# Sharing idle V columns between steps, leaving out the idle lane, and a new order of work, in a two-lane transformer kernel on TensorE

## The chip, the cores and the metric

The kernel runs on one core of one Trainium2 chip. The metric is the device time of a run in microseconds (us).

Engines in the views: PE is TensorE's matmuls, PEld its weight loads, DVE is VectorE, ACT is ScalarE, POOL is GpSimd, SP issues the transfers.

## The reference, cut to what matters

```python
def _A_ref(x, wqkv, wo):         # 32 heads of 18; token s sees s, s-2, ... s-14 (8 places)
    logits = jnp.einsum('bhsd,bhswd->bhsw', q, kg) * scale
    attn = _softmax(logits)
    o = jnp.einsum('bhsw,bhswd->bhsd', attn, vg)
    return o @ wo
def _B_ref(x, mem0, Wq, Wk, Wv, Wo, seg_len):   # 32 heads of 128, segments of 32, memory of 8
    mem = mem0
    for s in range(n_seg):                      # 64 segments, one after another
        h = concatenate([mem, x[segment s]])    # 40 tokens
        o = softmax(q k' * scale, masked) v @ Wo
        mem = o[:, :8]; outs.append(o[:, 8:])
x = A_x                                         # 2048 tokens of 576
x = x + _A_ref(_layernorm(x), A_wqkv, A_wo)
x = x + _B_ref(_layernorm(x), ...)
x = x + _A_ref(_layernorm(x), A_wqkv, A_wo)
x = x + _B_ref(_layernorm(x), ...)
```

The memory makes layer B serial: a segment needs the memory tokens that the segment before it has made.

## The kernel before

The two B layers run side by side as two "lanes", lane 1 six segments behind lane 0. One step `t` treats one segment of each lane: 80 columns in `hT`, in the order x of lane 0 (32), memory of lane 0 and of lane 1 (16), x of lane 1 (32). There are 70 steps; the first six have lane 0 alone, the last six lane 1 alone. The 64 tiles of layer A (64 tokens each) fill the gaps. A planner in the program simulates the engines with given durations and fixes the order of every engine's instructions from the priorities given with each operation.

Layer A has no matmul for its local attention: GpSimd multiplies q with eight shifted k into a large tile `big`, TensorE sums over channels, and after the softmax the weights are spread over the channels again ("spread"), evicted into `big`, multiplied by v on VectorE and added up, mostly on GpSimd.

```python
# tile of layer A: the product on GpSimd
def prod(e, c0=c0, nb=nb):
    self.tt(e, big.t[:, c0:c0 + nb], qT.t[...].to_broadcast([P, nb, AW, T]), win(kT.t, c0, nb), ALU.mult)
o = pl.op("POOL", 1.0 * nb + 0.05, prod, pr(0.34 + 0.02 * n), ...)
# [cut: logits, softmax] the spread, and its evictions by ScalarE or VectorE (AD_)
ps = pl.buf("o4")
b = pl.op("PE", 0.35, lambda e, ps=ps: spread(ps, 0, 4), pr(0.55), [o], acq=[ps], ...)
for g in range(NQ):
    evs.append(pl.op(AD_, _evac(512), lambda e, g=g, ps=ps: self.copy(e, big.t[:, 0:4, :, g * 16:(g + 1) * 16],
                                                                      ps.t[:, g, :]...), pr(0.56), [b], ...))
# [cut] the first add of the products with v
o = pl.op(("POOL", "DVE"), (2.6, 0.85), lambda e: self.tt(e, big.t[:, :, 0:4], big.t[:, :, 0:4], big.t[:, :, 4:8], ALU.add), ...)
# [cut] the normalised tokens xnb; the upper half of one block is a copy of the lower
o = pl.op("DVE", 0.18, lambda e: nc.vector.tensor_copy(out=xnb.t[64:128, :, 5, :], in_=xnb.t[0:64, :, 4, :]), ...)
# a step's tokens into hT
self.x_in[t][l] = pl.op(("POOL", "DVE"), (0.45, 0.2),
    lambda e, l=l, s=s, xnb=xnb: self.copy(e, hT.t[:, :, XC[l]:XC[l] + SEG], xnb.t[:, s % NS]), ...)
# V of block b (32 of the 96 columns of hT), two halves of 20 matmuls
for r in range(2):
    ps = pl.buf("r")
    def mm(e, r=r, ps=ps):
        for kc in range(5):
            for c in range(4):
                ...  l = hT.t[:, kc, b * 32:b * 32 + 32]
                nc.tensor.matmul(ps.t[c * 32:(c + 1) * 32, :], lhsT=l, rhs=w, start=(kc == 0), stop=(kc == 4))
# softmax of a step: sums, 1/sum, product (for the memory's queries "em" on VectorE)
nc.vector.tensor_reduce(out=s, in_=v, axis=AX.X, op=ALU.add)
nc.vector.reciprocal(out=s, in_=s)
if mul == "DVE":
    nc.vector.tensor_tensor(out=v, in0=v, in1=s...to_broadcast(shp), op=ALU.mult)
```

Of the kernel before, what the change touches and what calls it, by code (L numbers as in the profile page):

```python
# [16 lines left out]
P = 128  # L17
SEG = 32
NM = 8
W80 = 80  # L20
# [10 lines left out]
AW = 8  # L31
# [163 lines left out]
class _K:  # L195
# [37 lines left out]
    def setup(self):  # L233
# [110 lines left out]
        tiles("em", 2, [P, 4, 96], zero=True)  # L344
        tiles("ex", 2, [P, 2, 4, 64], zero=True)
# [3 lines left out]
        nc.gpsimd.memset(self.OT[:], 0.0)  # L349
        self.pl.pool("OTm", [None])  # L350
        self.pl.pool("OTx", [None])
        tiles("qk", 7, [P, 3, 2, W80])
# [32 lines left out]
    def layernorm(self, xT, dep, prio, writer, wus, wacq=(), wuses=()):  # L385
# [3 lines left out]
        a = pl.op(AD_, (0.46, 0.49), lambda e: self.copy(e, xs.t[:, :, 0, :], xT.t[:]), prio, [dep], acq=[xs], uses=[xT])  # L389
# [6 lines left out]
        b = pl.op(AD_, (0.46, 0.49), square, prio, [a], uses=[xs, xT])  # L396
# [6 lines left out]
        c = pl.op("PE", 0.28, mm, prio, [b], acq=[ps], uses=[xs])  # L403
# [16 lines left out]
    def wblock(self, i, prio, dep):  # L420
        w = self.pl.buf("ring")
        o = self.pl.op("SP", 0.5, lambda e: self.nc.sync.dma_start(out=w.t[:], in_=self.wA[i]), prio, [dep], acq=[w], lat=3.2)
        return w, o

    def a_tile(self, layer, j, dep, due, span):
# [4 lines left out]
        def pr(f):  # L430
            return due - span * (1.0 - f)
        if layer == 1:
# [21 lines left out]
        gate = pl.op("NONE", 0.0, None, pr(0.1), [o_x], acq=[xn])  # L454
        o_n = self.layernorm(xT, gate, pr(0.1), wr, 1.67, wuses=[xn])
# [5 lines left out]
        for part in (0, 1, 2):  # L461
            ps = pl.buf("r")
            o = o_n
            for c in range(5):
                w, ow = self.wblock(part * 5 + c, pr(0.2) - 0.1, gate)
# [5 lines left out]
                o = pl.op("PE", 0.15, mm, pr(0.22 + 0.03 * part), [o, ow], acq=[ps, dst[part]] if c == 0 else (),  # L471
                          uses=[xn, w] if c == 0 else [xn, w, ps], lat=0.0 if c < 4 else None)
                if c == 0 and part > 0:
                    def hcopy(e, part=part):
                        h = dst[part].t[:, :, 0:HALO]
                        if first:
                            nc.gpsimd.memset(h, 0.0)
                        else:
                            nc.gpsimd.tensor_copy(out=h, in_=hin[0].t[:, part - 1])
                    got[part, "h"] = pl.op("POOL", 0.25, hcopy, pr(0.22), [o] if first else [o, hin[1]],  # L480
                                           uses=[dst[part]] if first else [dst[part], hin[0]])
# [7 lines left out]
            got[part] = pl.op(AD_, _evac(320), ev, pr(0.24 + 0.03 * part), [o], uses=[ps, dst[part]])  # L489
        if j + 1 < self.NT:  # L490
# [5 lines left out]
            oh = pl.op("POOL", 0.5, hsave, pr(0.33), [got[1], got[2]], acq=[hk], uses=[kT, vT])  # L496
# [8 lines left out]
        for n, (c0, nb) in enumerate(((0, 2), (2, 2), (4, 1))):  # L505
# [3 lines left out]
            o = pl.op("POOL", 1.0 * nb + 0.05, prod, pr(0.34 + 0.02 * n), [o] if o else [got[0], got[1], got[1, "h"]],  # L509
# [10 lines left out]
        o = o_l = pl.op("PE", 0.4, logits, pr(0.5), [o], acq=[psL, e_], uses=[big], mode="C")  # L520

        def amax(e):
            v = psL.t[:, 0:P].rearrange("p (w t) -> p w t", w=AW)
            if first:
# [3 lines left out]
        o = pl.op("DVE", 0.6, amax, pr(0.5), [o], acq=[nmx], uses=[psL])  # L528
        o = pl.op("ACT", 0.28, lambda e: nc.scalar.activation(out=e_.t[:], in_=psL.t[:, 0:P].rearrange("p (w t) -> p w t", w=AW),
                                                              func=ACT.Exp), pr(0.5), [o], uses=[psL, e_])  # L530
# [5 lines left out]
        o = pl.op("DVE", 0.9, norm, pr(0.52), [o], acq=[ssum], uses=[e_])  # L536
# [8 lines left out]
        b = pl.op("PE", 0.35, lambda e, ps=ps: spread(ps, 0, 4), pr(0.55), [o], acq=[ps], uses=[e_], mode="R")  # L545
        evs = []
        for g in range(NQ):
            evs.append(pl.op(AD_, _evac(512),
                             lambda e, g=g, ps=ps: self.copy(e, big.t[:, 0:4, :, g * 16:(g + 1) * 16],
                                                             ps.t[:, g, :].rearrange("p (c w t) -> p c w t", c=4, w=AW)),  # L550
                             pr(0.56), [b], uses=[ps, big]))
        ps = pl.buf("o4")
        b = pl.op("PE", 0.1, lambda e, ps=ps: spread(ps, 4, 1), pr(0.58), [b], acq=[ps], uses=[e_], mode="R")
        e4 = pl.op(AD_, _evac(512),
                   lambda e, ps=ps: self.copy(e, big.t[:, 4].rearrange("p w (g t) -> p g w t", g=NQ),
                                              ps.t[:, :, 0:P].rearrange("p g (w t) -> p g w t", w=AW)),
                   pr(0.6), [b], uses=[ps, big])
        mus = []
        for c0, nb in ((0, 2), (2, 2), (4, 1)):
            mus.append(pl.op("DVE", 0.15 + 0.3 * nb,  # L560
                             lambda e, c0=c0, nb=nb: self.tt(e, big.t[:, c0:c0 + nb], big.t[:, c0:c0 + nb], win(vT.t, c0, nb), ALU.mult),
                             pr(0.62), evs + [got[2], got[2, "h"]] if nb == 2 else [e4, got[2], got[2, "h"]], uses=[big, vT]))
# [3 lines left out]
                  pr(0.64), mus, uses=[big])  # L566
        o = pl.op(PD, (1.44, 0.5), lambda e: self.tt(e, big.t[:, :, 0:2], big.t[:, :, 0:2], big.t[:, :, 2:4], ALU.add),
                  pr(0.66), [o], uses=[big])
        o = o_o = pl.op(PD, (0.78, 0.33), lambda e: self.tt(e, oT.t[:], big.t[:, :, 0], big.t[:, :, 1], ALU.add),
                        pr(0.68), [o], acq=[oT], uses=[big])  # L570
        ps = pl.buf("r")
        for mb in range(5):
            w, ow = self.wblock(WOB + mb, pr(0.68) - 0.1, o_l)

            def mm(e, mb=mb, w=w, ps=ps):
                for c in range(5):
                    nc.tensor.matmul(ps.t[:, mb * T:(mb + 1) * T], lhsT=w.t[:, c, :], rhs=oT.t[:, c, :], start=(c == 0), stop=(c == 4))
            o = pl.op("PE", 0.15, mm, pr(0.72), [o, ow], acq=[ps] if mb == 0 else (),
# [3 lines left out]
                  pr(0.75), [o], uses=[ps, xT])  # L582
# [5 lines left out]
        def wr2(e, m, rstd):  # L588
# [5 lines left out]
            for o, i, bc in views:  # L594
                self.tt(e, o, i, bc(m), ALU.subtract)
                self.tt(e, o, o, bc(rstd), ALU.mult)
        o = self.layernorm(xT, o, pr(0.8), wr2, 2.1, wacq=[xnb])
        o = pl.op("DVE", 0.18, lambda e: nc.vector.tensor_copy(out=xnb.t[64:128, :, 5, :], in_=xnb.t[0:64, :, 4, :]),
                  pr(0.9), [o], uses=[xnb])
# [43 lines left out]
    def softmax(self, ps, e_, n, prio, dep, mul, view, eview, last, pt, ptpool):  # L643
# [29 lines left out]
        if mul != "DVE":  # L673
# [6 lines left out]
            "p i b q -> p (i b q)" if len(pt.t.shape) == 4 else "p l i b q -> p (l i b q)"), in_=e_.t[:].rearrange(  # L680
            "p i k -> p (i k)" if len(e_.t.shape) == 3 else "p l i k -> p (l i k)")), prio, [o], acq=[pt], uses=[e_])

    def load_x(self, t):
# [7 lines left out]
        for l in range(2):  # L691
            s = self.lane_seg(t, l)
            if s is None:
                continue
            xnb, dep = self.xn_ready[l][s // NS]
            self.x_in[t][l] = pl.op(("POOL", "DVE"), (0.45, 0.2),
                                    lambda e, l=l, s=s, xnb=xnb: self.copy(e, hT.t[:, :, XC[l]:XC[l] + SEG], xnb.t[:, s % NS]),
                                    t - 0.42, [dep, gate], uses=[hT, xnb])
            if s == 0:
# [5 lines left out]
    def qk(self, t, g, prio):  # L705
# [4 lines left out]
        hT, ps, sb = self.hT[t], pl.buf("r"), pl.buf("qk")  # L710

        def mm(e):
            pv = ps.t[:, 0:480].rearrange("p (h w k) -> p h w k", h=3, w=2)
            for hh, h in enumerate(heads):
                for wi in range(2):
                    wt, wr = self.Wb[wi]
                    for kc in range(4):
                        nc.tensor.matmul(pv[:, hh, wi, :], lhsT=wt[:, kc, h * P:(h + 1) * P], rhs=hT.t[:, kc, 0:W80],  # L718
                                         start=(kc == 0), stop=False)
                    nc.tensor.matmul(pv[:, hh, wi, :], lhsT=wr[:, (h % 16) * P:(h % 16 + 1) * P],  # L720
                                     rhs=hT.t[:, 4 + h // 16, 0:W80], start=False, stop=True)
        o = pl.op("PE", 0.358 * n, mm, prio, [*self.x_in[t].values(), *self.mem_in[t]], acq=[ps, sb], uses=[hT], tmin=TW[0])
# [3 lines left out]
        def ev(e):  # L726
            pv = ps.t[:, 0:480].rearrange("p (h w k) -> p h w k", h=3, w=2)
            self.copy(e, sb.t[:, 0:n], pv[:, 0:n])
        self.qk_ev[g] = pl.op(AD_, _evac(160 * n), ev, prio, [o], uses=[ps, sb])
        self.qkt[g] = sb  # L730

    def vpass(self, t, b, prio):

        nc, pl = self.nc, self.pl
        hT, V = self.hT[t], pl.buf(f"V{b}")
        wv, wvr = self.Wb[2]
        self.V[b] = V
        xin = [self.x_in[t][0 if b == 0 else 1]]
        gate = pl.op("NONE", 0.0, None, prio, xin, acq=[V])
        for r in range(2):  # L740
            ps = pl.buf("r")

            def mm(e, r=r, ps=ps):
                for kc in range(5):
                    for c in range(4):
                        if kc < 4:
                            l, w = hT.t[:, kc, b * 32:b * 32 + 32], wv[:, kc, (16 * r + 4 * c) * P:(16 * r + 4 * c + 4) * P]
                        else:
                            l, w = hT.t[:, 4 + r, b * 32:b * 32 + 32], wvr[:, 4 * c * P:(4 * c + 4) * P]
                        nc.tensor.matmul(ps.t[c * 32:(c + 1) * 32, :], lhsT=l, rhs=w, start=(kc == 0), stop=(kc == 4))  # L750
            o = pl.op("PE", 1.08, mm, prio, [gate] + (self.mem_in[t] if b == 1 else []), acq=[ps], uses=[hT, V],
# [4 lines left out]
    def scores(self, t, r, kind, prio):  # L756
# [6 lines left out]
        e_, pt = pl.buf("e" + kind), pl.buf("pt" + kind)  # L763
        self.e_[kind] = e_
# [5 lines left out]
        def mm(e):  # L770
# [12 lines left out]
            for l in range(1 if m else 2):  # L783
                for i in range(4):
# [251 lines left out]
```

## Time and profile before

| | before |
|---|---|
| time, median of three runs | 2670.16 us (2659.29 to 2672.51) |
| TensorE busy, share of the span | 88% |
| VectorE busy | 67% |
| GpSimd busy | 34% |
| matmuls | 73360 |
| steps with both lanes (6 to 63), per pair of steps | 72.8 us |

The last row, and all times of stretches below, come from the timeline: VectorE's copy of the new memory (`hT<-psY`) closes each step, and I take the distance of such copies.

Columns after the bar: busy time in us, mean ns of one, idle time before.

```profile
L671 DVE TENSOR_TENSOR em<-em,sum 128x320 bf16<-128x320 bf16 x140 | 71.6, 511 | 4.8
L598 DVE COPY xnb<-xnb 64x64 bf16<-64x64 bf16 x64 | 16.8, 298 | 2.9 <-POOL xnb L230 1.8
```

The typical copy in the timeline lasts 0.17 us; a mean of 298 ns says that some last longer: 20 of the 64 take over 0.4 us, most of them about 0.5. The excess adds up to some 6 us (16.8 - 64 x 0.17) in the whole run.

### The profile page before, as it was taken

The page shows a single profiled execution, that of the slowest core. Times are in us where ns is not written, and L with a number is a line of the kernel's source. Part 1 is how long each engine was busy: PE and PEld are TensorE (multiplying, and loading weights), DVE is VectorE, ACT ScalarE, POOL GpSimd, SP SyncE. Part 2 cuts the span into 40 slices and gives each one's busy share as a digit, 9 for nine tenths or more (in the row PEclk, how much of TensorE's full clock was granted, in tenths as well). Part 3 has the DMA queues.
Part 4 walks back from the last instruction along what each step waited for, and adds up shares of the span by engine and source line. Part 5 has one row for each costly group of instructions (what it writes and reads, how often), then busy time and mean ns, then how long its engine had stood idle before and what let it go on. Part 6 is the DMA issues. An engine that isn't in the chain of part 4 may idle for free.

```text
span 2673.1 us, 158511 instructions
## 1 busy us (share of the span) xinstructions
PE 2348.8 (88%) x73360; PEld 1975.7 (74%) x73360; DVE 1783.3 (67%) x4094; ACT 942.6 (35%) x2048; POOL 913.2 (34%) x1250
## 2 busy tenths in 40 slices
PE   0279899989999999999999999999999999999998
PEld 0167777777787777777787787777777777777777
DVE  1256777667777667766767676767776667676665
ACT  0022333333333334333333333434343334333322
POOL 3222333333343433333333343433333333332220
PEclk9999999999999999999999999999999999999999
DMA  7721333333333333333333333333333333322210
GB/s 257 196 85 57 101 95 88 104 105 98 100 105 114 114 114 103 97 90 107 102 111 102 100 106 114 114 114 101 95 92 103 109 104 96 103 76 62 61 42 8
DMA packets 231420, 270.45 MB, mean 101 GB/s; under 512 B 42340, under 2 KB 227236, under 8 KB 229220
## 3 DMA queue, kind: packets, MB, share of 16 engines
q1 hardware_dynamic: 227508, 241.44, 31.0%
q0 software_dynamic: 3248, 18.88, 2.0%
q8 instruction: 573, 9.39, 1.5%
q14 instruction: 91, 0.75, 0.1%
HBM read 244.10 MB, written 16.12 MB: 97 GB/s over the span
## 4 chain that ended last, share of the span: by engine, by line
PE 67%; DVE 11%; ACT 7%; DMA 6%; issue 3%; SPq 3%; POOL 2%; ACTq 0%; DVEq 0%; POOLq 0%
PE r L718 21%; PE r L750 14%; PE psY L865 12%; DMA ring<-wA_blk 6%; PE r L720 5%; PE r L469 5%; DVE big L225 3%; ACT big L223 3%; PE o L841 2%; SPq L298 2%; ACT OT L223 2%; PE o L808 2%; DVE r L659 2%; DVE nmx L658 1%; PE o L542 1%
## 5 line engine op out<-in xcount | busy, mean ns | idle before, releaser
L718 PE MATMUL r<-hT,wq 128*128 128x80 bf16 x8960 | 695.2, 202 | 0.5 <-ACT em L661 0.2
L718 PE MATMUL r<-hT,wk 128*128 128x80 bf16 x8960 | 694.9, 202 | 0.0
L750 PE MATMUL r<-wv,hT 128*32 128x512 bf16 x6720 | 447.7, 384 | 56.8 <-ACT em L661 33.6
L718 PEld LDWEIGHTS <-wq 128*128 128x128 bf16 x8960 | 461.4, 100 | 36.8 <-issue 33.2
L865 PE MATMUL psY<-OT,wo 128*128 128x80 bf16 (+1 forms) x11360 | 451.7, 202 | 19.4 <-issue 8.2
L718 PEld LDWEIGHTS <-wk 128*128 128x128 bf16 x8960 | 466.2, 100 | 0.0
L720 PE MATMUL r<-hT,wk_r 128*128 128x80 bf16 x2240 | 453.2, 202 | 0.0
L720 PE MATMUL r<-hT,wq_r 128*128 128x80 bf16 x2240 | 453.1, 202 | 0.0
L865 PEld LDWEIGHTS <-wo 128*128 128x128 bf16 x11360 | 428.4, 100 | 29.1 <-issue 27.0
L225 DVE CAST qk<-r 128x480 bf16<-128x480 f32 (+1 forms) x409 | 262.6, 642 | 259.4 <-PE r L720 256.3
L230 POOL TENSOR_TENSOR ex<-ex,sum 128x384 bf16<-128x384 bf16 x140 | 115.9, 828 | 864.5 <-DVE sum L669 790.4
L750 PEld LDWEIGHTS <-hT 128*32 128x32 bf16 x8400 | 211.1, 97 | 241.7 <-issue 84.7
L230 POOL TENSOR_TENSOR big<-qT,kT 128x1024 bf16<-128x1024 bf16 (+1 forms) x192 | 326.0, 1705 | 140.2 <-ACT kT L223 48.6
L223 ACT ACTIVATE qk<-r 128x480 bf16<-128x480 f32 (+1 forms) x361 | 200.7, 557 | 182.6 <-PE r L720 181.9
L469 PE MATMUL r<-xn,ring 128*128 128x64 bf16 x4800 | 237.4, 196 | 26.0 <-DMA ring<-wA_blk 18.0
L223 ACT ACTIVATE OT<-o 128x512 bf16<-128x512 f32 (+1 forms) x335 | 163.3, 507 | 243.0 <-PE o L841 101.5
L230 POOL TENSOR_TENSOR big<-big 128x640 bf16<-128x640 bf16 (+1 forms) x62 | 93.1, 1501 | 417.5 <-DVE big L230 407.4
L469 PEld LDWEIGHTS <-ring 128*128 128x128 bf16 x4800 | 181.5, 99 | 66.9 <-issue 33.3
L720 PEld LDWEIGHTS <-wk_r 128*128 128x128 bf16 x2240 | 224.5, 100 | 0.0
L720 PEld LDWEIGHTS <-wq_r 128*128 128x128 bf16 x2240 | 224.4, 100 | 0.0
L223 ACT ACTIVATE V<-r 128x512 bf16<-128x512 f32 x250 | 149.2, 597 | 208.5 <-PE r L750 206.8
L750 PE MATMUL r<-wv_r,hT 128*32 128x512 bf16 x1680 | 169.7, 382 | 0.8 <-issue 0.8
(137 smaller groups left out, 3501.5 us busy)
## 6 DMA issues: line engine op xcount, KB each, us to landing
ring<-wA_blk SPq DMA_DIRECT2D x1280, 160.0 KB, 3.0
x1T<-x SPq DMA_DIRECT2D x32, 160.0 KB, 3.6
x<-x1T SPq DMA_DIRECT2D x32, 160.0 KB, 2.4
x3T<-x SPq DMA_DIRECT2D x32, 160.0 KB, 3.9
x<-x3T SPq DMA_DIRECT2D x32, 160.0 KB, 3.7
wo<-in_B_Wo_dram POOLq DMA_DIRECT2D x1, 4608.0 KB, 27.5
wq<-in_B_Wq_dram POOLq DMA_DIRECT2D x4, 1024.0 KB, 10.8
wk<-in_B_Wk_dram POOLq DMA_DIRECT2D x4, 1024.0 KB, 20.1
```

Of the source, the lines that this page charges most:

```text
L223: nc.scalar.activation(out=out, in_=in_, func=ACT.Copy, scale=1.0 if scale is None else scale)
L225: (nc.vector if e == "DVE" else nc.gpsimd).tensor_copy(out=out, in_=in_)
L230: (self.nc.vector if e == "DVE" else self.nc.gpsimd).tensor_tensor(out=out, in0=in0, in1=in1, op=op)
L298: nc.sync.dma_start(out=self.wA[i], in_=wn[:, :, col0:col0 + P])
L469: nc.tensor.matmul(ps.t[:, c * T:(c + 1) * T], lhsT=w.t[:, kc, :], rhs=xn.t[:, kc, :], start=(kc == 0), stop=(kc == 4))
L659: nc.vector.tensor_tensor(out=v, in0=v, in1=m.unsqueeze(len(shp) - 1).to_broadcast(shp), op=ALU.add)
L718: nc.tensor.matmul(pv[:, hh, wi, :], lhsT=wt[:, kc, h * P:(h + 1) * P], rhs=hT.t[:, kc, 0:W80], start=(kc == 0), stop=False)
L720: nc.tensor.matmul(pv[:, hh, wi, :], lhsT=wr[:, (h % 16) * P:(h % 16 + 1) * P], rhs=hT.t[:, 4 + h // 16, 0:W80], start=False, stop=True)
L750: nc.tensor.matmul(ps.t[c * 32:(c + 1) * 32, :], lhsT=l, rhs=w, start=(kc == 0), stop=(kc == 4))
L808: nc.tensor.matmul(ps.t[:, c, i * 16:(i + 1) * 16], lhsT=V[b].t[q4, r, i, :], rhs=pt.t[q4, i, b, 0:16], start=(i == 0 and b == 0), stop=(i ...
L841: nc.tensor.matmul(o, lhsT=V[b].t[q4, r, i, :], rhs=p, start=(r == 0 and i == 0 and b == 0), stop=(r == 1 and i == 3 and b == 2), skip_gro ...
L865: nc.tensor.matmul(psY.t[:, mb, c0:], lhsT=self.wo[:, w0:w0 + P], rhs=self.OT[:, h, c0:], start=(h == 0 and mb == 0), stop=(h == NH - 1 an ...
```

## The change

Three V passes of 32 columns per step carry 80 columns of tokens: 16 columns are empty. The change puts 16 tokens of lane 0's next segment there in even steps, so that the odd step needs two passes, five per pair in place of six. Steps with one lane compute only their own columns (Q, K, scores, PV, output projection). And all priorities of the planner get new values, weights of A are requested earlier, and the spread is evicted by channel block.

```diff
@@ V passes
+    def vblocks(self, t):
+        l0, l1 = self.lanes(t)
+        if t % 2 == 0:
+            return [(0, 0) if l0 else None, (1, 32), (2, 64) if l0 or l1 else None]
+        return [(2, None) if l0 else None, (1, 16), (0, 48) if l1 else None]
...
-   l, w = hT.t[:, kc, b * 32:b * 32 + 32], wv[...]
+   l, w = hT.t[:, kc, c0:c0 + 32], wv[...]
@@ tokens of the next segment
+            if l == 0 and t % 2 == 0:
+                self.x_ahead = pl.op(("POOL", "DVE"), (0.25, 0.17), lambda e, ...:
+                                     self.copy(e, hT.t[:, :, W80:HW_], xnb.t[:, s % NS + 1, :, 0:HW_ - W80]), ...)
@@ Q and K, output projection: only the columns of the lanes that are on
+        a, b = 0 if l0 else 40, W80 if l1 else 40
...
+        c0, c1 = (0 if on[0] else MC if m else XC[1]), (W80 if on[1] else XC[1])
@@ spread of A
-        for g in range(NQ):
-            evs.append(... big.t[:, 0:4, :, g * 16:(g + 1) * 16] <- ps.t[:, g, :] ...)
+        for c in range(5):
+            if c == 4:
+                ps = pl.buf("o4")
+                b = pl.op("PE", 0.1, lambda e, ps=ps: spread(ps, 4, 1), pr(Q[4] + 0.02), [b], ...)
+            evs.append(... big.t[:, c] <- ps.t[:, :, c % 4 * P:(c % 4 + 1) * P] ..., pr(Q[4] + 0.01 * c), ...)
@@ priorities (before: numbers in place)
+PR = dict(qk=0.07, qkd=0.043, v1=0.432, v0=0.542, m0=0.196, x0=0.393, m1=0.369, x1=0.577, pm0=0.625, pm1=0.332,
+          o=0.747, od=0.01, mo=0.789, xo=1.046, px=1.007, v2=0.838, a1=0.606, a1s=3.252, a2=1.206, a2s=1.532,
+          fin=4.369, res=-0.44, ring=1.183, A=(0.005, 0.238, 0.614, 0.586, 0.529, 0.726, 0.636, 0.949))
```

(Cut: score and PV index work, wider softmax tiles, the order of heads in OT, a layernorm whose square no longer waits for its copy, memsets, durations given to the planner.)

## The prediction

> **What bounds the kernel now.** I read the head of the page first, then the costliest groups, then TensorE's waits, then one pair of steps by stretch and by time.
>
> ```profile
> span 2673.1 us, 158511 instructions
> PE 2348.8 (88%) x73360; PEld 1975.7 (74%) x73360; DVE 1783.3 (67%) x4094; ACT 942.6 (35%) x2048; POOL 913.2 (34%) x1250
> ...
> PE 67%; DVE 11%; ACT 7%; DMA 6%; issue 3%; SPq 3%; POOL 2%; ACTq 0%; DVEq 0%; POOLq 0%
> PE r L718 21%; PE r L750 14%; PE psY L865 12%; DMA ring<-wA_blk 6%; PE r L720 5%; PE r L469 5%; DVE big L225 3%; ACT big L223 3%; PE o L841 2%; SPq L298 2%; ACT OT L223 2%; PE o L808 2%; DVE r L659 2%; DVE nmx L658 1%; PE o L542 1%
> ```
>
> TensorE is busy 88% of the span, 104 us of the rest being set-up before its first matmul, and two thirds of the chain that ended last is its work. The reader is to see that it is the bound nearly everywhere, so a matmul removed should be time removed. The kernel is 70 steps of the memory layer ("B"), with the tiles of the local-attention layer ("A") as filler between. Steps 0 to 5 have only lane 0, 6 to 63 both lanes, 64 to 69 only lane 1. VectorE's copy of the new memory into hT marks the ends of steps: one stands at 1282.19 us, the next but one at 1354.86. That stretch, one pair of steps, in the view by stretches (columns: stretch, length, then busy us of PE, PEld, DVE, ACT, POOL):
>
> ```profile
> 1282.19:1354.86 72.67, 67.11 (x2124) 56.70 (x2121) 51.27 (x120) 28.16 (x62) 27.27 (x36) 1.00 0.36 103
> ```
>
> So 72.7 us a pair, DVE at 51.3 of them (71%), clock at full: no second engine is near its limit. 5.6 us per pair TensorE sits idle. The view of waits, TensorE alone, between 360 and 2440 us (28.5 pairs), says for whom (total us, times, longest):
>
> ```profile
> PE o L841 <- DVE big L225: 33.1, 28, 1.4
> PE r L750 <- ACT em L661: 31.1, 55, 1.0
> PE o L542 <- DVE big L225: 21.6, 28, 0.8
> PE o L841 <- issue: 15.4, 15, 2.1
> PE r L469 <- DMA ring<-wA_blk: 12.8, 22, 2.2
> PE r L750 <- ACT V L223: 11.7, 28, 0.4
> ```
>
> The same few waits come back in every pair: 28 and 55 times are once and twice a pair.
>
> The price of one matmul is read from the timeline, as the distance from one start to the next; the durations on the page (202 ns for one of 80 columns) overlap.
>
> ```profile
> 1341.77 1.05 PE L750 MATMUL r<-wv,hT 128*32 128x512 bf16 x16
> 1342.64 0.39 PE L750 MATMUL r<-wv_r,hT 128*32 128x512 bf16 x4
> 1342.86 0.31 PE L781 MATMUL r<-mask_m,ident 128*32 128x320 bf16 x4
> ...
> 1344.38 0.41 PE L791 MATMUL r<-qk 128*32 128x48 bf16 x32
> 1344.72 0.51 PE L808 MATMUL o<-ptm,V 32*128 32x16 bf16 x48
> 1345.19 0.31 PE L469 MATMUL r<-xn,ring 128*128 128x64 bf16 x5
> ...
> 1351.35 0.31 PE L469 MATMUL r<-xn,ring 128*128 128x64 bf16 x5
> 1351.50 0.88 PE L865 MATMUL psY<-OT,wo 128*128 128x80 bf16 x20
> ...
> 1352.51 2.31 PE L865 MATMUL psY<-OT,wo 128*128 128x80 bf16 x60
> 1354.65 0.86 PE L469 MATMUL r<-xn,ring 128*128 128x64 bf16 x15
> 1355.45 0.93 PE L841 MATMUL o<-ptx,V 32*128 32x32 bf16 x96
> 1356.31 0.47 PE L469 MATMUL r<-xn,ring 128*128 128x64 bf16 x10
> ```
>
> Half a V pass (20 matmuls): 1342.86 - 1341.77 = 1.09 us. 80 columns: 2.14 us / 60 = 35.7 ns. 64 columns: 0.15 / 5 = 30 ns. Scores of 48 columns: 0.34 / 32 = 10.6 ns. PV of the memory: 0.47 / 48 = 9.8 ns; PV of x: 0.86 / 96 = 9.0 ns.
>
> **What the Trainium skill says.** "TensorE: Matmul & The Clock Gate", section "Back-to-back issue gap": columns / 2.4 + 2.5 ns when warm, with a floor of about 25 ns from 64 columns down. The trace agrees at 80 (35.8 against 35.7) and at 64 (29.2 against 30); this case has no 40-column matmul yet to show the floor. The same page's section on packing small matmuls says that tiles in different column groups run at once: 512 columns take 215.8 ns by the formula, and the trace does four such V matmuls in 218. "TensorEngine Tiling (Array Packing)", section "Key Properties", says that a change of tiling mode drains the engine; the trace has about 0.1 us at such places. "Perfetto Trace Analysis", section "Identifying the Most-Contended Engine", calls matmul busy time a bad measure because matmuls are pipelined; that is why I count by starts.
>
> **The change, part by part.** Counts are from the instruction streams of both kernels as built.
>
> 1. V passes. A two-lane step computed V in three 32-column passes. Now an even step does three, the third taking the first 16 tokens of lane 0's next segment in columns 80 to 95, and the odd step reuses that tile and does two. One-lane steps do only what they need. Passes: 29 pairs x 5 + 12 + 12 = 169 in place of 210. Matmuls 8400 to 6760; 82 halves x 1.09 us = 89 us. Their 82 evictions go too, off TensorE.
> 2. Q and K of the 12 one-lane steps: 3840 matmuls go from 80 to 40 columns. Between the floor of 25 ns and the 30 ns measured at 64 I take 29 ns as an estimate, since each also loads 128 x 128 weights: 3840 x 6.7 ns = 26 us.
> 3. Output projection: 1920 matmuls go from 80 to 48 or 16 columns: 13 us by the same price.
> 4. Scores: 384 fewer x 10.6 ns = 4 us. PV: 288 x 9.8 + 384 x 9.0 ns = 6 us.
> Together 138 us of TensorE issue time.
> 5. The order. All priorities have new values, weights of A are asked for earlier, and A's spread softmax is evicted by channel block rather than token group, so that the product with v starts when its own block is out. In the new order of a steady pair, 50 or 60 Q/K matmuls stand between the two spreads (1.8 to 2.1 us, enough for two rounds of 0.6 to 0.7 us evictions), 30 more between the last spread and PV of x, and a V half goes into the free third PSUM buffer after the scores where it used to wait for the exponential. Each answers a wait listed above. The named ones without "issue" sum to 110 us. I count on 65%, some 70 us: a wait removed exposes the next.
> 6. Costs: a few more memsets and an extra small copy per pair. One 2.2 us memset goes and seven of some 0.5 us come on the set-up path: 2 us. V dependencies of the odd step reach back a step, but that tile is a step old when used. One-lane odd steps are now so short (20 to 21 us of matmuls) that the serial chain shows. From scores to transposed probabilities the last steps show 4.6 us on VectorE and ScalarE; the new order puts some 2.6 to 3.9 us of matmuls there. With the start-up, where A's first tiles are awaited, I give back 8 us.
>
> Sum: 2670 - 138 - 70 + 10 = 2472; I say 2470.
>
> **Rivals.** (a) Subtraction alone: the new order is no better, its waits come back elsewhere. 2670 - 138 + 10 = 2540. For it: the waits have many causes and three PSUM buffers remain. Against: the new order visibly fills the very places. (b) The order works fully: 2670 - 138 - 110 = 2420. Against: "issue" waits and drains remain. (c) The serial chain (Q/K, scores, softmax, PV, projection, memory copy) becomes the bound of one-lane steps. The late ones take 29.5 us now; if they can't go below 26, about 2 us more are lost in each of 12 steps: 2495. (d) Narrow matmuls are held by their weight load at nearly 35 ns: 35 us less gain, 2505. Against: 64 columns already run at 30. (e) VectorE or GpSimd becomes the bound: 71% and 37% busy in a pair, and VectorE loses most V evictions; I give this little.
>
> **Range and chances.** Between (b) and (a) lies nearly everything: 2415 to 2540. To miss 2% the time would have to stay above 2617, i.e. under 40% of the pure subtraction. Faster 0.97, within 2% 0.02, slower 0.01.
>
> **What would show it.** TensorE's matmuls in V: 6760 with an unchanged distance of 1.09 us per half. A steady pair near 68.5 us (72.7 - 2.2 for the V pass - 2 for order). Waits of PV of x and of the spread on "big" gone or under 10 us, waits on the exponential near nil. 40-column matmuls about 29 ns apart. One-lane late steps near 24 us. I am wrong if the steady pair stays above 70 us (order gave nothing), below 66 (it gave all), or if one-lane steps keep over 27 us with TensorE idle behind the softmax.

## The result, and the profile after

| | before | after |
|---|---|---|
| median, same rounds | 2665.72 us (2659.29 to 2672.51, 4 runs) | 2558.97 us (2553.12 to 2568.25, 4 runs) |
| matmuls | 73360 | 70664 |
| VectorE busy | 1783.3 us (67%) | 1837.9 us (72%) |

The ratio is 0.9602, with a 95% interval of 0.9561 to 0.9644. Ratios are computed from the mean time of one kernel's fast runs over that of the other's of the same rounds, so they differ slightly from the ratio of the medians quoted. The change makes the kernel 4.0% faster; predicted were 7.5%, and 2559 us lies outside the predicted 2415 to 2540.

Where the time went, from the copies that close the steps in both profiled runs (us):

| stretch | before | after | difference |
|---|---|---|---|
| start to the end of step 0 | 191.9 | 176.3 | -15.6 |
| steps 1 to 5, lane 0 alone | 168.2 | 140.9 | -27.3 |
| steps 6 to 63, both lanes | 2110.1 | 2067.3 | -42.8 |
| steps 64 to 68, lane 1 alone | 162.0 | 132.9 | -29.1 |
| rest | 40.9 | 34.1 | -6.8 |

So the parts with one lane gained 79 us, and the 29 pairs with both lanes only 43 us: 1.5 us a pair, from 72.8 to 71.3. The prediction wanted 68.5, and named a pair above 70 us as a sign of being wrong. The whole shortfall is in the steady steps.

The page of the kernel after, its head and its chain of waits by engine:

```profile
span 2551.4 us, 153085 instructions
PE 2198.3 (86%) x70664; PEld 1865.3 (73%) x70664; DVE 1837.9 (72%) x4066; ACT 885.3 (35%) x1993; POOL 954.7 (37%) x1289
...
PE 60%; DVE 23%; ACT 6%; issue 5%; SPq 3%; POOL 1%; DMA 1%; DVEq 0%; ACTq 0%; POOLq 0%
```

The reader is to see that VectorE's busy time grew by 55 us, although it has fewer instructions (4066 for 4094), and that its share of the chain doubled from 11% to 23%. An engine that is busier with fewer instructions is one whose instructions became longer in the mean.

A steady pair by stretch, between two of the closing copies (columns as in the prediction):

```profile
1322.58:1394.25 71.67, 65.12 (x2082) 55.44 (x2078) 54.89 (x120) 26.89 (x60) 28.41 (x37) 1.00 0.37 106
```

VectorE does as many instructions as in the pair before, 120, in 54.9 us where it took 51.3. TensorE still idles 6.6 us.

TensorE's waits between 360 and 2350 us (total us, times, longest):

```profile
PE r L726 <- DVE qk L225: 45.7, 26, 2.9
PE o L543 <- ACT big L223: 31.5, 52, 1.4
PE r L575 <- DVE oT L230: 15.1, 22, 0.8
PE o L840 <- DVE ptm L681: 12.6, 24, 1.5
```

The waits that the prediction listed are gone, as far as their names go: PV of x on `big`, 33.1 us before, is 0.4; V on `em` is not in the list; the weight ring went from 12.8 to 1.3 us between these times (from 18.0 to 7.4 in the whole run). But these four sum to 105 us, and the five of before summed to 110. At the top stands a wait that did not exist: Q/K matmuls (L726) wait for VectorE to evict the Q/K tile before. The spread's wait has only changed its name: from VectorE's eviction (21.6, once a pair) to ScalarE's (31.5, nearly twice a pair).

### Why the eviction of Q/K is late

One of these 26 waits, in the timeline of all engines (start, duration, engine, line, operation, output<-input):

```profile
1365.53 3.92 POOL L230 TENSOR_TENSOR big<-qT,kT 128x1024 bf16<-128x1024 bf16 x2
...
1366.64 2.88 DVE L596 COPY xnb<-xnb 64x64 bf16<-64x64 bf16 x1
...
1369.56 0.21 DVE L225 COPY hT<-xnb 128x192 bf16<-128x192 bf16 x1
1369.68 1.22 DVE L225 CAST qk<-r 128x480 bf16<-128x480 f32 x2
1370.38 0.30 PE L726 MATMUL r<-hT,wq 128*128 128x80 bf16 x4 [1.95 <-DVE qk L225]
```

A copy of 64 x 64 values that lasts 0.17 us at other times lasts 2.88 us. It ends at 1369.52, just after GpSimd's two products have ended at 1369.45. (Of the 28 xnb copies that take over 0.4 us in this trace, 12 waited for one GpSimd instruction and 16 for two or three.) Behind it on VectorE's queue stand the evictions of Q/K; the PSUM tiles stay full, and TensorE stands still for 1.95 us. By shape, in the kernel after:

```profile
L673 DVE TENSOR_TENSOR em<-em,sum 128x320 bf16<-128x320 bf16 x140 | 109.4, 782 | 4.8
L596 DVE COPY xnb<-xnb 64x64 bf16<-64x64 bf16 x64 | 62.2, 972 | 7.1 <-POOL xnb L230 5.2
L225 DVE COPY hT<-xnb 128x192 bf16<-128x192 bf16 x32 | 27.4, 856 | 1.0
```

The mean of the copy went from 298 to 972 ns, that of the product with 1/sum from 511 to 782 ns, while the typical (median) instruction kept its 0.17 and 0.49 us. A mean that moves while the median stays is the sign of instructions held up now and then. The Trainium skill has the reason in "SBUF — State Buffer", section "Who interferes with whom": VectorE and GpSimd share one pair of SBUF ports as an exclusive lock; copies and casts in a fast mode, and VectorE instructions with two SBUF inputs, contend for it; a `tensor_reduce` never does, nor does an instruction with at most one SBUF input outside those modes. The prediction did not look this page up. These profiles fit it; the experiments below test it.

### Why the spread still waits

The four evictions of a first spread, and the second spread (same timeline, lines of other work left out):

```profile
1343.68 0.69 DVE L225 CAST big<-o 128x512 bf16<-128x512 f32 x1 [0.22 <-PE o L543]
...
1344.41 0.60 ACT L223 ACTIVATE big<-o 128x512 bf16<-128x512 f32 x1 [0.53 <-DVE big L225]
...
1345.11 0.69 DVE L225 CAST big<-o 128x512 bf16<-128x512 f32 x1 [0.73 <-ACT big L223]
...
1345.83 0.60 ACT L223 ACTIVATE big<-o 128x512 bf16<-128x512 f32 x1 [0.83 <-DVE big L225]
...
1346.48 0.24 PE L543 MATMUL o<-e,epadT 32*128 32x128 bf16 x4 [1.02 <-ACT big L223]
```

Though two engines share them, each waits for the one before it: 2.75 us in a row (1343.68 to 1346.43). The program as built carries these waits. The prediction had put them in two rounds of 0.6 to 0.7 us, with both engines at once, and so found 1.8 to 2.1 us of matmuls enough to hide them.

### The profile page after: what moved, and what is told of

Read it like the earlier page. It is cut to its first block, busy times and chain, and to the rows that moved or that the text cites. A ratio compares the mean times of both kernels' runs of the same rounds, so it can differ in the third digit from the quotient of the medians.

```text
span 2551.4 us, 153085 instructions
## 1 busy us (share of the span) xinstructions
PE 2198.3 (86%) x70664; PEld 1865.3 (73%) x70664; DVE 1837.9 (72%) x4066; ACT 885.3 (35%) x1993; POOL 954.7 (37%) x1289
## 4 chain that ended last, share of the span: by engine, by line
PE 60%; DVE 23%; ACT 6%; issue 5%; SPq 3%; POOL 1%; DMA 1%; DVEq 0%; ACTq 0%; POOLq 0%
PE r L726 18%; PE psY L912 12%; PE r L771 9%; PE r L470 5%; PE r L728 4%; DVE big L225 3%; ACT big L223 3%; DVE r L661 3%; DVE big L230 3%; SPq L298 2%; PE o L878 2%; DVE nmx L660 2%; DVE xnb L596 2%; DVE qk L225 2%; DVE em L673 2%
## 5 line engine op out<-in xcount | busy, mean ns | idle before, releaser
L726 PE MATMUL r<-hT,wq 128*128 128x80 bf16 (+1 forms) x8960 | 676.1, 199 | 67.7 <-DVE qk L225 45.7
L726 PE MATMUL r<-hT,wk 128*128 128x80 bf16 (+1 forms) x8960 | 675.6, 199 | 2.7 <-issue 2.5
L726 PEld LDWEIGHTS <-wq 128*128 128x128 bf16 x8960 | 458.2, 99 | 128.9 <-issue 115.7
L912 PE MATMUL psY<-OT,wo 128*128 128x80 bf16 (+3 forms) x11360 | 443.3, 199 | 22.3 <-issue 13.7
L726 PEld LDWEIGHTS <-wk 128*128 128x128 bf16 x8960 | 453.9, 100 | 5.1 <-issue 4.9
L728 PE MATMUL r<-hT,wq_r 128*128 128x80 bf16 (+1 forms) x2240 | 445.0, 199 | 2.0 <-issue 2.0
L728 PE MATMUL r<-hT,wk_r 128*128 128x80 bf16 (+1 forms) x2240 | 445.2, 199 | 1.0 <-issue 1.0
L771 PE MATMUL r<-wv,hT 128*32 128x512 bf16 x5408 | 360.9, 383 | 8.6 <-issue 7.2
L225 DVE CAST qk<-r 128x480 bf16<-128x480 f32 (+3 forms) x395 | 232.1, 593 | 139.3 <-PE r L728 134.5
L223 ACT ACTIVATE qk<-r 128x480 bf16<-128x480 f32 (+3 forms) x375 | 194.5, 528 | 188.3 <-PE r L728 187.4
L470 PEld LDWEIGHTS <-ring 128*128 128x128 bf16 x4800 | 184.2, 99 | 45.7 <-issue 24.7
L223 ACT ACTIVATE OT<-o 128x512 bf16<-128x512 f32 (+1 forms) x220 | 106.0, 497 | 184.2 <-PE o L878 106.7
L223 ACT ACTIVATE big<-o 128x512 bf16<-128x512 f32 x169 | 100.2, 597 | 193.3 <-PE o L543 118.7
```

The lines of the kernel that those rows point to most:

```text
L223: nc.scalar.activation(out=out, in_=in_, func=ACT.Copy, scale=1.0 if scale is None else scale)
L225: (nc.vector if e == "DVE" else nc.gpsimd).tensor_copy(out=out, in_=in_)
L470: nc.tensor.matmul(ps.t[:, c * T:(c + 1) * T], lhsT=w.t[:, kc, :], rhs=xn.t[:, kc, :], start=(kc == 0), stop=(kc == 4))
L726: nc.tensor.matmul(pv[:, hh, wi, a:b], lhsT=wt[:, kc, h * P:(h + 1) * P], rhs=hT.t[:, kc, a:b], start=(kc == 0), stop=False)
L728: nc.tensor.matmul(pv[:, hh, wi, a:b], lhsT=wr[:, (h % 16) * P:(h % 16 + 1) * P], rhs=hT.t[:, 4 + h // 16, a:b], start=False, stop=True)
L912: nc.tensor.matmul(psY.t[:, mb, c0:c1], lhsT=self.wo[:, w0:w0 + P], rhs=self.OT[:, h % 16 // 4 * 8 + h // 16 * 4 + h % 4, c0:c1], start=(h ...
```

## The experiments

Theory 1 ("shared port"): the new order makes VectorE's small copies fall into GpSimd's long products; they hold up the evictions behind them, and that ate most of the expected gain. Theory 2 ("order or subtraction"): the new order is worth little, or work taken away in the steady steps doesn't count any more because another engine sets the pace. Theory 3 ("evictions in a row"): the second spread waits because the evictions are serial. All kernels below gave correct results. For comparison across chips, the tables give the ratio to the kernel before in the same rounds; one thousandth is 2.7 us.

### First round: the parts of the change, and the copies elsewhere

**old_order**: the changed kernel with the values of the priorities that stood in the kernel before.

```diff
-PR = dict(qk=0.07, qkd=0.043, v1=0.432, ... A=(0.005, 0.238, 0.614, 0.586, 0.529, 0.726, 0.636, 0.949))
+PR = dict(qk=0.05, qkd=0.045, v1=0.36, ... A=(0.1, 0.22, 0.34, 0.5, 0.55, 0.62, 0.72, 0.8))
```

> The changed kernel with the old kernel's priorities written back in; all skipped work stays skipped, the other small edits stay. Prediction's theory (the new order is worth some 70 us): about 2630 us. Theory Port (the new order removes the old waits but places VectorE's copies and two-operand products under long GpSimd instructions, which block them, so that the order is worth about nothing in a steady pair): 2545 to 2575 us, no more than 1% from the changed kernel, with the old waits of PV of x and of V back and the wait of Q/K on the qk eviction gone.

**three_passes**: three V passes again in steps with both lanes; new priorities, one-lane parts kept.

```diff
-        if t % 2 == 0:
+        if t % 2 == 0 or (l0 and l1):
             return [(0, 0) if l0 else None, (1, 32), (2, 64) if l0 or l1 else None]
(cut: the index work that follows from it)
```

> The changed kernel with three V passes in every two-lane step again; order values and narrow one-lane steps stay. If a V pass is worth its matmuls, 2.2 us for each of 29 pairs: 2559 + 63 = 2622 us. If the freed time is only eaten by waits on VectorE that were there anyway: 2560 to 2590 us.

**copies_act**: the copies that VectorE makes from SBUF to SBUF (xnb, and tokens into hT) made by ScalarE, at the same places of the plan. TensorE's and GpSimd's orders are identical to those of the changed kernel.

```diff
-        o = pl.op("DVE", 0.18, lambda e: nc.vector.tensor_copy(out=xnb.t[64:128, :, 5, :], in_=xnb.t[0:64, :, 4, :]),
+        o = pl.op("DVE", 0.18, lambda e: self.copy("ACT", xnb.t[64:128, :, 5, :], xnb.t[0:64, :, 4, :]),
...
-   lambda e, l=l, s=s, xnb=xnb: self.copy(e, hT.t[...], xnb.t[:, s % NS]),
+   lambda e, l=l, s=s, xnb=xnb: self.copy("ACT" if e == "DVE" else e, hT.t[...], xnb.t[:, s % NS]),
```

> The changed kernel with the small bf16 SBUF-to-SBUF copies of VectorE (64 into the upper half of xnb, 35 into hT) issued on ScalarE at the same place of the plan; the order on TensorE is untouched. Theory Port: the blocked time of these copies (some 70 us of VectorE) goes, the wait of Q/K on VectorE's qk eviction (45.7 us) falls under 15 us, time 2505 to 2530 us. Rival (the shortfall is the order of VectorE's own work and the serial evictions, not blocking): within 12 us of the changed kernel, 2559.

**pool_split**: GpSimd's products cut into pieces (about 0.6 us each in the trace), its first add into five, all in place.

```diff
-                self.tt(e, big.t[:, c0:c0 + nb], qT.t[:, c0:c0 + nb]..., win(kT.t, c0, nb), ALU.mult)
+                for b0 in range(c0, c0 + nb):
+                    for w0 in range(0, AW, 4):
+                        ...  self.tt(e, big.t[:, b0:b0 + 1, w0:w0 + 4], qT.t[:, b0:b0 + 1]..., k_[:, :, w0:w0 + 4], ALU.mult)
(cut: the add)
```

> The changed kernel with GpSimd's long products and its long add cut into pieces of about 0.5 us, same place in the plan. Theory Port: a blocked VectorE instruction then waits for a piece, not for 2 to 4 us; the mean of the product em with sum falls from 782 to under 600 ns, of the copy into xnb from 972 to under 450 ns, and the time to 2500 to 2535 us although GpSimd has more to do. Rival (no blocking): 2559 to 2585 us, the extra GpSimd instructions costing a little.

| run | median us | ratio to before (95%) | both-lane pair, us |
|---|---|---|---|
| before | 2655.92 | 1 | 72.8 |
| after (own rounds) | 2558.97 | 0.9602 (0.9561 to 0.9644) | 71.3 |
| old_order | 2636.64 | 0.9936 (0.9903 to 0.9970) | 74.7 |
| three_passes | 2713.98 | 1.0225 (1.0197 to 1.0254) | 77.0 |
| copies_act | 2499.01 | 0.9421 (0.9391 to 0.9451) | 69.7 |
| pool_split | 2566.85 | 0.9672 (0.9647 to 0.9697) | |

What follows. The two parts don't add: taking work away in the old order leaves 0.6%, and the new order with the old number of passes is worse than before. Part of old_order's mean pair of 74.7 is one step of 98.7 us at the start of the second lane, in which TensorE waits for the first A tiles; without it a pair is some 72.6, no better than before, although 40 matmuls a pair are gone. So the priorities fit this set of work, and an order taken over from other work can lose all that the work saved. This speaks against reading theory 2 as a simple sum.

Both runs missed figures that were put down for them. old_order's ratio is 2649 us on the scale of 2666: near the 2630 of the prediction's theory, though 64 of the 89 us between it and the changed kernel are the one long step (98.7 us for 34.6), and far from theory 1's 2545 to 2575. It isn't free of hold-ups either: its 14 VectorE copies of 16 columns into hT have a mean of 1610 ns. three_passes is 2726 us on that scale, where 2622 was the highest figure, so it doesn't give the price of a V pass. Its mean granted clock was 0.951, against 0.990 in the kernel after, and most of its pairs have a stretch like this one (length, then busy us of the engines; after them the granted clock, 0.50):

```profile
1046.65:1053.47 6.82, 6.15 (x175) 5.89 (x172) 3.29 (x10) 1.09 (x4) 3.73 (x6) 0.50 0.66 194
```

If the clock was either full or half, these means make some 270 us at half clock in three_passes and 50 in the kernel after (an estimate: 2 x (1 - 0.951) x 2718, and 2 x (1 - 0.990) x 2551). TensorE's work takes up to 110 us longer by that, beside the 63 us of added matmuls; the difference between the two kernels is 166. So a good part of what three_passes lost can be the clock; why it is lower there was not tested.

Moving the copies, with TensorE's order untouched, gained 1.8 points, and the wait of Q/K on VectorE's `qk` fell from 45.7 to 0.2 us. That fits theory 1, but also "VectorE had too much to do", since it has less work then; that stays to be told apart.

pool_split missed: it is 0.7 points slower than the changed kernel. The pieces let some copies in and not others. One that they didn't (timeline of the run, both engines):

```profile
1372.08 4.78 POOL L230 TENSOR_TENSOR big<-qT,kT 128x256 bf16<-128x256 bf16 x8
...
1373.20 3.87 DVE L600 COPY xnb<-xnb 64x64 bf16<-64x64 bf16 x1
```

The copy starts in the second of eight pieces and ends at 1377.07, after the last of them at 1376.86. It waited for the whole run of instructions back to back, not for the one that was running. The same can be seen above, where the copy waited through two products. But it isn't the rule. The copies into hT, held for a whole product in the changed kernel, went from 856 to 388 ns:

```profile
L225 DVE COPY hT<-xnb 128x192 bf16<-128x192 bf16 x32 | 12.4, 388 | 1.0
```

Of the 41 copies that take over 0.4 us in this trace, 24 ended with the piece that was running, though the next followed without a gap, and 17, nearly all of them xnb copies, waited through three to nine instructions; so the mean of the xnb copy rose from 972 to 1176 ns. What decides between the two isn't shown. The product em x 1/sum did get in between pieces at times: its mean fell from 782 to 684 ns. GpSimd's busy time grew from 955 to 1045 us.

### Second round: blocked or overloaded, and what TensorE's time is worth

**copies_reduce**: the same copies stay on VectorE, at the same place, but as a maximum over an axis of length one, which copies the values. Orders of TensorE and GpSimd are identical.

```diff
-   nc.vector.tensor_copy(out=xnb.t[64:128, :, 5, :], in_=xnb.t[0:64, :, 4, :])
+   nc.vector.tensor_reduce(out=xnb.t[64:128, :, 5, :], in_=xnb.t[0:64, :, 4, :].unsqueeze(3), axis=AX.X, op=ALU.max)
(the same for VectorE's copies of 32 columns into hT)
```

> The changed kernel with the small copies that VectorE makes from SBUF to SBUF (the upper half of xnb; tokens into hT) written as a maximum over an axis of length one: same values, same engine, same place in the order, only another kind of instruction. Theory 'shared port' (a copy on VectorE waits until GpSimd's running product has ended, a reduction doesn't): the copies take about 0.2 to 0.4 us each in the mean instead of 972 ns, and the time comes to 2490 to 2515 us, as when ScalarE took them. Theory 'VectorE has too much work': the work is the same or a little longer, so 2550 to 2570. Theory 'it was only the order on VectorE's queue' gives the same 2550 to 2570.

**v_twice**: the changed kernel, with one V pass of each odd both-lane step issued twice.

```diff
-                for kc in range(5):
+                for kc in [*range(5), *range(5)] if twice else range(5):   # twice: k == 1, t odd, both lanes on
```

> The changed kernel, with the matmuls of one V pass of each odd two-lane step issued twice in place: 29 x 40 matmuls x 54.5 ns = 63 us of TensorE issue more, nothing else moved, result unchanged. Theory 'TensorE still sets the pace in the steady steps': +55 to +65 us, 2615 to 2625 us. Theory 'VectorE or the softmax chain sets the pace there now, TensorE's idle time takes it up': under +35 us, below 2595.

**act_addsplit**: copies_act, with GpSimd's first add in five pieces.

```diff
-   lambda e: self.tt(e, big.t[:, :, 0:4], big.t[:, :, 0:4], big.t[:, :, 4:8], ALU.add)
+   lambda e: [self.tt(e, big.t[:, a_:b_, 0:4], big.t[:, a_:b_, 0:4], big.t[:, a_:b_, 4:8], ALU.add)
+              for a_, b_ in (((0, 1), (1, 2), (2, 3), (3, 4), (4, 5)) if e == "POOL" else ((0, 5),))]
```

> Copies on ScalarE, and GpSimd's first add of the spread product (128 x 1280[...]) cut into five of about 0.85 us in place, so that VectorE's normalising product of em gets in between. Theory 'the em product waits for the add': TensorE's wait of PV of the memory on ptm falls from 21 us to under 10, and the time from 2499 to about 2485. Theory 'a run of pieces back to back blocks like one long instruction' (as the copies did in the earlier experiment with pieces): no change, 2495 to 2505.

**act_ev2**: copies_act, with the four evictions of the first spread made as two of twice the size.

```diff
-            evs.append(pl.op(AD_, _evac(512), lambda e, c=c, ps=ps: self.copy(e, big.t[:, c]..., ps.t[:, :, c % 4 * P:(c % 4 + 1) * P]...), ...
+            c_, n_ = {0: (0, 2), 1: (0, 0), 2: (0, 0), 3: (2, 2), 4: (4, 1)}[c]
+            evs.append(pl.op(AD_, _evac(512), lambda e, c_=c_, n_=n_, ps=ps: n_ and self.copy(e, big.t[:, c_:c_ + n_]..., ps.t[:, :, c_ % 4 * P:(c_ % 4 + n_) * P]...), ...
```

> Copies on ScalarE, and the four evictions of the first spread, which run one after another, made as two of twice the size: TensorE's and GpSimd's orders are the same. Theory 'the four in a row are longer than the matmuls put behind them, so the second spread waits': two of about 1.0 and 1.2 us end about 0.4 us sooner than four of 0.65; the second spread's wait on big falls from 31 us to under 15, the time to about 2480. Theory 'that wait only stands in for another that comes after it': the wait falls, the time stays at 2495 to 2505.

| run | median us | ratio to before (95%) | both-lane pair, us |
|---|---|---|---|
| before | 2646.84 | 1 | 72.8 |
| copies_reduce | 2487.49 | 0.9386 (0.9353 to 0.9419) | 69.1 |
| v_twice | 2602.71 | 0.9825 (0.9790 to 0.9861) | 73.0 |
| act_addsplit | 2501.45 | 0.9437 (0.9409 to 0.9466) | |
| act_ev2 | 2478.27 | 0.9352 (0.9329 to 0.9375) | 68.8 |

(The pair of before is that of the first profile, in all three tables. Pairs come from one profiled run each, on chips whose medians for the kernel before differ by up to 0.7%, so they are good to about 0.5 us.)

copies_reduce decides between blocked and overloaded. VectorE has the same instructions at the same places, and only their kind differs:

```profile
L596 DVE TENSOR_REDUCE xnb<-xnb 64x64 bf16<-64x64 bf16 x64 | 13.6, 213 | 7.4 <-POOL xnb L230 5.4
L699 DVE TENSOR_REDUCE hT<-xnb 128x192 bf16<-128x192 bf16 x32 | 11.2, 351 | 1.0
```

A single copy is now a little slower (0.21 for 0.17 us, 0.35 for 0.21), none is held up, and the 96 of them take 25 us in place of 90. The kernel gains 2.2 points on the changed one, at least as much as with ScalarE's help. The overload theory asked for no gain. So the held-up copies cost (0.9602 - 0.9386) x 2666 = 58 us, with an uncertainty of some 14 from the two intervals; by the profiled traces the 29 pairs lost 2067.3 - 2002.7 = 65 us to them.

v_twice: 0.9825 - 0.9602 is 2.2 points or 59 us (again some 15 either way; 49 us by the pairs of the two traces) for 63 us of added matmuls. So in the changed kernel most of a V pass's time is still time of the kernel (its clock, 0.991, is that of the changed kernel, so this run is a fairer price than three_passes). TensorE's work sets the pace, with waits in between; work taken away in the steady steps does count. This rules out theory 2 in the form "another engine sets the pace".

act_addsplit: no gain. (The add took 2.61 us before, its pieces 0.69 each.) The product's mean fell from 780 to 683 ns, TensorE's wait for `ptm` only from 21.3 to 17.5 us, and the time didn't move. Neither theory's figure for the wait was met; the cutting let some products in, not all.

act_ev2: the two evictions in the timeline, and TensorE's wait that remained:

```profile
1308.08 1.22 DVE L225 CAST big<-o 128x1024 bf16<-128x1024 f32 x1 [0.22 <-PE o L543]
```

```profile
PE o L543 <- ACT big L223: 15.4, 25, 0.6
```

The second, on ScalarE, ran from 1309.40 to 1310.42, so the row lasted 2.34 us where four took 2.75. The wait fell from 31.2 us in 51 cases to 15.4 in 25, and the time by (0.9421 - 0.9352) x 2656 = 18 us, with intervals that don't overlap. Theory 3 holds. It wasn't merely a wait in place of another. The two evictions were not tried in the kernel before, whose spread also waits on such a row (21.6 us), so this gain isn't shown to be special to the change.

### Third round: both remedies, a control, and the product

**red_ev2**: copies_reduce and act_ev2's two evictions together (copies on VectorE as reductions).

> The two remedies together: VectorE's copies as reductions, and the four evictions of the first spread as two. TensorE's order unchanged. If the two costs are separate, the gains add: 2559 - 60 (copies as reductions) - 18 (evictions) = about 2475 on the scale of the changed kernel's 2559, a ratio of about 0.932 to the kernel before. If one wait only stood in for the other, the ratio stays at 0.935 to 0.939.

**before_red**: the kernel before, with the same copies as reductions.

```diff
-   nc.vector.tensor_copy(out=xnb.t[64:128, :, 5, :], in_=xnb.t[0:64, :, 4, :])
+   nc.vector.tensor_reduce(out=xnb.t[64:128, :, 5, :], in_=xnb.t[0:64, :, 4, :].unsqueeze(3), axis=AX.X, op=ALU.max)
(and the copies into hT)
```

> Control: the kernel before, with the same copies written as reductions. In its trace these copies were held behind GpSimd for only some 10 us in all and TensorE waits on none of them by name. Theory 'the blocking came with the new order': the time stays within 1% of before, ratio 0.993 to 1.003. Theory 'the copies cost both kernels the same, so the change itself was not hurt by them': ratio 0.975 to 0.98.

**red_ev2_es**: red_ev2, with 1/sum of the memory's softmax in unused columns of the PSUM tile of the scores. All orders are those of red_ev2.

```diff
-            s = bc(ss, shp)
+            s = ps.t[:, 480:484] if mul == "DVE" else bc(ss, shp)
```

> red_ev2 with the sums of the memory's softmax put into unused columns of the PSUM tile of the scores, so that the product em x 1/sum reads one operand from PSUM; order of all engines unchanged, but the PSUM tile is held until that product is done. Theory 'two operands from SBUF is what makes the product wait for GpSimd': its mean falls from 781 ns to about 500 or less (a little over its own time alone), TensorE's wait for ptm from 20 us to under 8, time down by 10 to 15 us. Theory 'any VectorE product on SBUF data waits': mean stays near 780. If V's matmuls then wait for the PSUM tile, the gain is given back.

| run | median us | ratio to before (95%) | both-lane pair, us |
|---|---|---|---|
| before | 2655.83 | 1 | 72.8 |
| red_ev2 | 2469.25 | 0.9309 (0.9282 to 0.9335) | 68.5 |
| before_red | 2652.62 | 0.9999 (0.9974 to 1.0024) | 72.2 |
| red_ev2_es | 2495.63 | 0.9412 (0.9381 to 0.9443) | |

The control settles where the copies' cost comes from: the same edit is worth nothing in the kernel before. The hold-ups that cost time came with the change. For the xnb copy they need both its parts: with the old order and the new work its mean is 294 ns, with the new order and three passes 289 ns, with both 972. The copies of 32 columns into hT are held in part in each of these (639, 597 and 856 ns, against 265 before).

red_ev2 is the fastest of all kernels here, 3% faster than the changed one (0.9309 / 0.9602 = 0.970). The gains nearly add (0.9602 - 0.0216 - 0.0069 = 0.9317). Its steady pair, by stretch:

```profile
1310.18:1378.98 68.80, 65.04 (x2082) 55.38 (x2080) 51.34 (x117) 27.44 (x59) 28.57 (x37) 1.00 0.38 110
```

TensorE's busy time, 65.0 us, is that of the pair above; VectorE's is back from 54.9 to 51.3, and what went from the pair is idle time alone.

red_ev2_es shows the port rule once more, and why it is no remedy here:

```profile
L673 DVE TENSOR_TENSOR em<-em,r 128x320 bf16<-128x320 bf16 x140 | 68.2, 487 | 4.8
```

```profile
PE r L470 <- DVE em L673: 37.1, 27, 1.5
```

With one operand in PSUM the product is no longer held: 777 ns fell to 487, and the wait for `ptm` from 18.9 to 7.0 us, as expected. But the PSUM tile now stays taken until that product is done, and A's projections, next in line for it, wait 37.1 us that were not there. The kernel lost a point. So a held-up product was cheaper than a PSUM tile kept longer; what the product's hold-up costs by itself isn't measured.

## Why the prediction was wrong, by its own steps

- **Steps 1 to 4, work taken away: right, in part too low.** V's matmuls are 6760 as counted. Q/K of 40 columns are 25.0 ns apart where I took 29: ten groups of five between these two starts, 1.25 us.

```profile
2479.96 0.25 PE L726 MATMUL r<-hT,wk 128*128 128x40 bf16 x4
...
2481.21 0.25 PE L726 MATMUL r<-hT,wk 128*128 128x40 bf16 x4
```

  So step 2 was 3840 x 10.7 = 41 us, not 26. The output projection at 48 columns has its 80 matmuls 25 ns apart, by their starts, so step 3 was low as well. The parts with one lane gained 79 us where these steps, less the 10 us of cost, gave about 65 for them (26 for 24 V halves, 26, 13, 10, minus 10). Of the five late one-lane steps three take 22.8 to 24.8 us (29.5 to 31.1 before) and two take 31 (35 and 36 before); "near 24" was right for the three, and rival (c), the serial chain, lost: TensorE is busy 20.8 of 22.8 us in one of the three, and the two longer ones have more matmuls (27.8 of 30.6 us busy in the first, 26.4 of 31.3 in the other).
- **Step 5, the order: the failed step.** "I count on 65%, some 70 us." The steady pairs gained 43 us in all. Taken at the predicted price the V passes there (58 halves x 1.09) are worth 63, and v_twice shows that a V pass still costs 49 to 59 of 63 in the changed kernel. So the order, what it brought and what it spoiled together, cost about 6 to 20 us where a gain of 70 was counted on. Counted the other way, from old_order (72.6 a pair without its long step, 71.3 here), it gained some 38; the parts don't add, and either way it is far from 70. The rule of thumb behind it, that a wait removed exposes the next, was the right thought with the wrong size: the listed waits went and 105 us of others came.
- **What stood in its place, first: rival (e), "I give this little".** I argued from VectorE's busy share. The engine was not full. It was held: copies of 0.17 us stretched to as much as 4 us behind GpSimd's products, which by theory 1's test (copies_reduce) cost 58 us. A busy share counts the holding as work, and the page on SBUF that states the lock was not looked up.
- **What stood in its place, second: the evictions.** "Enough for two rounds of 0.6 to 0.7 us evictions" was a misreading. The four run in a row, in the kernel before too, where the timeline has them at 1315.27, 1315.90, 1316.62 and 1317.25. Shortening the row by 0.4 us gave 18 us.
- **The sum closes.** With both costs removed the steady pair is 68.5 us, the predicted figure, and the time is 2469 us on a chip where before took 2656 (0.9309; predicted 2470 / 2670 = 0.925). The agreement is partly luck: narrow matmuls gave more than reckoned, and some waits for `ptm` and the rest of the evictions remain.
- **Step 6** was wrong in direction for the start: it gave back 10 us for memsets, the serial chain and the start-up together, and the stretch to the end of step 0 fell by 15.6 us. The first matmul came at 103 us before (the prediction says 104) and at 104 after, so the memsets can have cost about 1 us, not 2.
- **Still open:** why these priorities and the reduced work together bring the copies into GpSimd's product, beyond the fact that they do; when a held copy gets in between two GpSimd instructions and when not; whether two evictions would have sped up the kernel before too; and the cost of the held em product.

## What to carry to other kernels

Before reordering a kernel, list the instructions of VectorE and GpSimd that contend for SBUF ports, and ask where each will fall in the new order; an engine's busy share says nothing of it, but a mean far over the median of one shape does. Where a small copy gets held, write it as an instruction that doesn't take the lock, and cutting the other engine's instruction up may not help. When a wait is to be hidden behind other work, check in the timeline whether the instructions awaited run side by side or in a row.

## What the Trainium skill lacked or had wrong

- "SBUF — State Buffer", section "Who interferes with whom", says that the loser is blocked until the other's instruction finishes. In pool_split that fits 24 of the 41 held VectorE copies; 17 waited on through three to nine GpSimd instructions (3.87 us for the one shown, though each piece took about 0.6 us). That this can happen, and when, isn't said.
- The same section states that a `tensor_reduce` never contends, and the runs agree (64 copies, mean 972 ns as copies, 213 ns as reductions over an axis of length one). That this makes a cheap remedy, 58 us in this kernel for 0.04 to 0.14 us more per copy, isn't said. That one operand in PSUM frees a product of two agrees as well (777 to 487 ns).
- "Perfetto Trace Analysis", section "Identifying the Most-Contended Engine", warns of matmul busy time, but calls the busy share a fair measure for VectorE. Here it wasn't: 65 us of VectorE's busy time was holding (90 us for 96 copies that need 25).
- "TensorE: Matmul & The Clock Gate", section "Back-to-back issue gap", says that its formula under-counts for narrow matmuls in a stream with weight loads. Here, with a new 128 x 128 weight for each matmul, it held at 80 columns (35.7 ns against 35.8), and at 40 the spacing was the section's floor of about 25 ns (25.0), which I should have trusted. At 64 columns, which its table puts at the floor too, the trace has 30.
